# First MLP by Horner's rule with h read from PSUM, GpSimd's arithmetic moved to VectorE

## The chip, the cores and the metric

The kernel runs on one core of one Trainium2 chip. The metric is the device time of one execution in microseconds. All arithmetic is in float32; a product that TensorE forms is made of three matmuls, with each operand split into a rounded high part and a low part (float32r).

## The reference

A linear recurrence over 768 steps in each of 4 x 8 heads gives x, and two MLPs follow, one on the other's result:

```
mag = sqrt(a_re^2 + a_im^2);  a <- a * min(mag, 0.999) / (mag + 1e-6)     # complex
S_re, S_im <- a * S + k v^T  (each step t; kv goes to the real part)
y[t] = q[t] . S_re                                   # [4, 8, 768, 48] -> x [3072, 384]

h = x @ w_in                                         # [3072, 2048]
g = (a0 + a1 h + a2 h^2 + a3 h^3) / (1 + |b0| |h| + |b1| h^2 + 1e-6)
x1 = g @ w_out                                       # [3072, 384]

out = (silu(x1 @ w_gate) * (x1 @ w_val)) @ w_out2    # d_ff = 1536
```

## The kernel before

The 3072 tokens are cut into 12 units of 256 tokens. For each unit an element-wise part works on VectorE, ScalarE and GpSimd: `ew_seed` (the magnitudes' seeds), `ew_scan` (products of the factors), `ew_q` and `ew_k` (the scaled q and k, stored to DRAM by `products`). An attention-like part, `at_units`, then works on chunks of 128 tokens: `at_pre` makes masked products `pm`, `at_post` carries the state `S` and writes x^T into the two parts `xh` and `xl` of a block.

A block is two units, 512 tokens; there are six. For each block `moe` runs the first MLP, 16 steps of 128 columns of d_ff, and the second MLP, 12 steps. One step of the first MLP: `up` makes `ph` = h in PSUM with nine matmuls (L182 to L184); ScalarE and VectorE evaluate numerator `u` and denominator `w`; `r` near 1/w comes from Ln and Exp on ScalarE (L122); `divide` makes `hi` (rounded quotient) and `lo` (its rest); `down` adds nine matmuls to the three accumulators `acc` (L190 with `hi`, L191 with `lo`, L192 with the weights' low part and `hi`). `divide` of a step is called in the step after it (`HALF = 1`), and its `down` one step later again (`pend`, `flush`). A step of the second MLP makes `pg` and `pv` with 18 matmuls, Silu on ScalarE (tile `u`), `z = pv * sg` on VectorE (L270, tile `w`), `hi` on ScalarE (L271) and `lo = z - hi` on GpSimd (L272); its `down` comes after the next step's `up`. The tiles `u`, `w` and `r` have three buffers, `hi` and `lo` two.

After each step `tick` calls the generators of other work, the element-wise part of units two blocks ahead and the attention of the next block, so that it is spread between the steps. Blocks 4 and 5 have no element-wise work left, block 5 no attention. The order on each engine is what the Tile framework's scheduler makes of the order of the calls and the dependencies; each engine then runs its own list in order. SyncE issues all the loads and stores.

In block 0 the weights come as float64 words. `converted` loads them, `to_bits` turns them into float32 with three VectorE instructions (L134 to L136), `narrow` rounds the high part on ScalarE (L143) and takes the low part on GpSimd (L146), and the two parts are stored to DRAM for the later blocks: 40 pieces, 28 of 768 columns and 12 of 384. `TOUCH` makes VectorE write one column of the destination first (L313). Other GpSimd work: `x + z` in `ew_seed` (L458) and `ew_k` (L559) for units 1 to 11, and for units 0 and 1 (`POOL_S`) the mask (L604), the state's sum (L620) and `xl` (L642).

Numerator and denominator of the first MLP are evaluated so:

```
u = a3 h + a2 (ScalarE);  s = h^2 (ScalarE);  w = b0 |h| (ScalarE)
u = u * s (GpSimd, L219);  w = s * b1 + w (VectorE, L220)
u = h * a1 + u (VectorE, L224, reads ph)
divide: hi = (u + a0) r (L232);  w = (w + 1 + eps) hi (L233)
        u = (u + a0) - w (L237);  lo = u r (L238), all VectorE
```

Of the kernel before, what the change touches and what calls it, by code (L numbers as in the profile page):

```python
# [37 lines left out]
POOL_S = range(2)  # L38
# [5 lines left out]
TOUCH = 1  # L44
# [9 lines left out]
LTR = [()] * 6  # L54
# [11 lines left out]
def tile_recurrence_moe(  # L66
# [63 lines left out]
    def to_bits(raw, x):  # L130
        """float64 words in raw to float32's bits in their lower halves; below the normal range these mean nothing."""
        words = raw.bitcast(I32).rearrange("p (n t) -> p t n", t=2)
        low, top = words[:, 0, :], words[:, 1, :]
        v_.tensor_scalar(x, top, 3, 0x3FFFFFFF, ALU.logical_shift_left, ALU.bitwise_and)  # L134
        stt(x, top, -0x40000000, x, ALU.bitwise_and, ALU.bitwise_or)
        stt(low, low, 29, x, ALU.logical_shift_right, ALU.bitwise_or)  # L136
        return top.bitcast(F32), low.bitcast(F32)

    def narrow(raw, x, wt, low_sum):
        """float64 words to float32 in the two parts of wt; low_sum > 0 if one is below the normal range."""  # L140
        t, xf = to_bits(raw, x)
        hi, lo = wt[:, 0, :], wt[:, 1, :]
        act(hi, xf, AF.Copy)  # L143
        act(t, t, AF.Abs)
        act(t, t, AF.Relu, scale=-1.0, bias=cst[:, 4:5], accum_out=low_sum)
        g_.tensor_tensor(lo, xf, hi.bitcast(F32), SUB)  # L146

    def narrow_any(raw, x, wt):
        """As narrow(), with what lies below the normal range taken as zero."""
        t, xf = to_bits(raw, x)  # L150
        act(t, t, AF.Abs)
        v_.tensor_scalar(t, t, WMIN, None, ALU.is_ge)
        tt(xf, xf, t, MUL)
# [19 lines left out]
    def moe(pools, T, x_hi, x_lo, out_ap, tick, middle, take, ltr=()):  # L173
        """x^T [128, KT, T] in two parts to out_ap [128, KT, T] in DRAM."""
# [24 lines left out]
        def flush(n):  # L199
            while len(pend) > n:  # L200
                down(*pend.pop(0))

        acc = [pacc.tile([128, T], F32, tag=f"acc{m}", name="acc") for m in range(KT)]
        for f in range(0, F1, gf):
# [6 lines left out]
            u, s, w, r = (mt(n) for n in ("u", "s", "w", "r"))  # L211
            hi, lo = mt("hi", F32R), mt("lo", F32R)
            L_ = f in ltr
            act(u, ph, AF.Identity, scale=a3, bias=a2)  # L214
            act(s, ph, AF.Square)  # L215
            act(w, ph, AF.Abs, scale=b0)  # L216
            if L_:
                act(r, ph, AF.Identity, scale=a1, bias=a0)
            g_.tensor_tensor(u, u, s, MUL)  # L219
            stt(w, s, b1, w, MUL, ADD)  # L220
            if L_:
                tt(u, u, r, ADD)
            else:
                stt(u, ph, a1, u, MUL, ADD)  # L224
            fact(r, w, AF.Ln, bias=cst[:, 2:3])
            fact(r, r, AF.Exp, scale=-1.0)

            def divide(L_=L_, f=f, wts=wts, u=u, w=w, r=r, hi=hi, lo=lo):
                if L_:
                    tt(hi, u, r, MUL)  # L230
                else:
                    stt(hi, u, a0, r, ADD, MUL)  # L232
                stt(w, w, 1.0 + EPS, hi.bitcast(F32), ADD, MUL)  # L233
                if L_:
                    tt(u, u, w, SUB)
                else:
                    stt(u, u, a0, w, ADD, SUB)  # L237
                tt(lo, u, r, MUL)  # L238
                for j in range(gf):
                    pend.append((acc, wts[j], DM, hi[:, j, :], lo[:, j, :], f + j == 0, f + j == F1 - 1))  # L240
# [17 lines left out]
        for f in range(0, F2, gf):  # L258
# [13 lines left out]
            g_.tensor_tensor(lo, z, hi.bitcast(F32), SUB)  # L272
            for j in range(gf):
                pend.append((acc2, wts[j], 0, hi[:, j, :], lo[:, j, :], f + j == 0, f + j == F2 - 1))
            flush(gf)
            tick(1)
# [26 lines left out]
    def converted(wp, src, scr, f):  # L303
        parts = []
        for c, n in spans(src):
# [6 lines left out]
            if TOUCH:  # L312
                v_.tensor_copy(wt[:, 0, 0:1], cst[:, 0:1])  # L313
# [20 lines left out]
    def general():  # L334
        """The recurrence a step at a time, where a product of its factors leaves float32's range."""
# [89 lines left out]
    with ExitStack() as es:  # L425
# [13 lines left out]
        def cmul(dst, x, y, t):  # L439
            """dst = x * y, all [128, 2, n]; t [128, 2, 2, n]."""  # L440
# [9 lines left out]
        def ew_seed(u):  # L450
# [7 lines left out]
            (g_ if u else v_).tensor_tensor(x, x, z, ADD)  # L458
# [60 lines left out]
        def products(u, i, src):  # L519
            """src * A, or src * A / |A|^2, to DRAM."""  # L520
# [13 lines left out]
        def chunk(u, n):  # L534
            """Q' and K' of a chunk as rows (part, d)."""
# [16 lines left out]
        def ew_k(u):  # L552
# [6 lines left out]
            (g_ if u else v_).tensor_tensor(x, x, z, ADD)  # L559
# [25 lines left out]
        def at_pre(u, n, held):  # L585
            """K'^T and the masked products of K' and Q' of a chunk."""
# [3 lines left out]
            for hh in range(2):  # L590
# [11 lines left out]
                if u in POOL_S:  # L602
                    act(pm, pp, AF.Copy)
                    g_.tensor_tensor(pm, pm, wide, MUL)  # L604
                else:
                    tt(pm, pp, wide, MUL)

        def at_post(u, n, held, xh, xl, col):
            st, vt, S_old = st_of.pop((u, n)), v_of.pop((u, n)), state[0]
            has_s = u % UPB > 0 or n > 0  # L610
            if "kT" in held:
# [5 lines left out]
                if u in POOL_S:  # L617
                    act(S_new, pg, AF.Copy)
                    if has_s:
                        g_.tensor_tensor(S_new, S_new, S_old, ADD)  # L620
                elif has_s:
# [16 lines left out]
            if u in POOL_S:  # L638
                xf = atp.tile([128, KT, 128], F32, tag="ysb", name="xf")
                act(xf, px, AF.Copy)  # L640
                act(xh[:, :, xs], px, AF.Copy)
                g_.tensor_tensor(xl[:, :, xs], xf, xh[:, :, xs].bitcast(F32), SUB)  # L642
            else:
                split(px, xh[:, :, xs], xl[:, :, xs])
# [12 lines left out]
        def at_units(*us):  # L657
            """Chunk by chunk, the first half of one beside the second half of the one before."""
# [45 lines left out]
        def merge(*streams):  # L704
            """(steps, their number) side by side, each spread over the whole."""
# [44 lines left out]
        for i in range(len(BLOCKS)):  # L750
# [43 lines left out]
            moe(pools, T, *xt[i], o, tick, silu, feed(stored, pools[3]) if i else first, LTR[i])  # L794
# [97 lines left out]
```

## Time and profile before

| | |
|---|---|
| three runs | 1402.33, 1409.41, 1424.78 us; median 1409.41 |
| profiled execution: span from first to last instruction | 1421.0 us |
| profiled execution's own time | not listed apart from the three runs; the slowest of them is 3.8 us above the span |
| TensorE matmuls busy | 1142.4 us, 80% |
| VectorE busy | 1142.4 us, 80% |
| ScalarE busy | 676.0 us, 48% |
| GpSimd busy | 408.2 us, 29%, 259 instructions |
| mean granted TensorE clock | 0.938 |

Busy time of an engine includes time in which an instruction has started and stands still. The sixteen DMA engines move 261.55 MB. The stages are told apart by the loads of activation tables: a first MLP needs Ln and Exp, a second one Silu. In order of time they are the start (0 to 170 us), then first and second MLP of blocks 0 to 5: 289.7, 422.1, 569.3, 671.9, 776.2, 870.9, 968.0, 1060.2, 1161.7, 1246.5 and 1333.1 us are the borders.

### The profile page before, as it was taken

Reading aid. Unit: us, or ns where it says so; the run is one execution under the profiler, and the core shown is the slowest. Engines: PE = TensorE matmul, PEld = TensorE weight load, DVE = VectorE, ACT = ScalarE, POOL = GpSimd, SP = SyncE. Lnnn points to the kernel's source line nnn. Section 1 sums busy time; section 2 is a strip of 40 time slices with the busy share of each in tenths; the row PEclk is TensorE's granted clock in tenths of the full one; section 3 lists DMA queues with packets and bytes.
Section 4 is the critical chain, followed back from the end, with each engine's and each line's share of the span. In section 5 each row is a group of like instructions: output and inputs, shape, how many; then the busy total and the mean of one; then the engine's idle time right before and its main releaser. Section 6 shows DMA issues by size and latency. Waiting matters only on the chain. (4 is left out here: it accounts for less than half of the span.)

```text
span 1421.0 us, 15576 instructions
## 1 busy us (share of the span) xinstructions
PE 1142.4 (80%) x5314; PEld 926.9 (65%) x5314; DVE 1142.4 (80%) x1878; ACT 676.0 (48%) x1078; POOL 408.2 (29%) x259
## 2 busy tenths in 40 slices
PE   0041977887679776999899998999989999988897
PEld 0041956675458455887678776788767888866686
DVE  7999689999897999799799896999987871159710
ACT  6454276864453647222865225763226542255421
POOL 2233354334441313022432223221222211123211
PEclk9999979988777997899899999999999999999999
DMA  7666254646565664667754676455756535544551
GB/s 268 231 214 199 94 158 167 212 166 228 199 199 212 170 213 155 195 216 215 242 162 146 206 234 207 156 180 192 226 182 199 163 110 178 170 143 158 181 170 47
DMA packets 129159, 261.55 MB, mean 184 GB/s; under 512 B 8112, under 2 KB 85168, under 8 KB 129072
## 3 DMA queue, kind: packets, MB, share of 16 engines
q1 hardware_dynamic: 129072, 260.47, 56.6%
q8 instruction: 44, 0.72, 0.2%
q14 instruction: 43, 0.35, 0.1%
HBM read 210.11 MB, written 50.33 MB: 183 GB/s over the span
## 5 line engine op out<-in xcount | busy, mean ns | idle before, releaser
L191 PE MATMUL acc<-lo,wt 128*128 128x512 f32 x504 | 220.1, 437 | 78.3 <-DVE lo L238 52.4
L219 POOL TENSOR_TENSOR u<-u,s 128x512 f32<-128x512 f32 x96 | 153.0, 1594 | 364.2 <-ACT s L215 329.4
L272 POOL TENSOR_TENSOR lo<-w,hi 128x512 fp32r<-128x512 f32 x72 | 104.1, 1446 | 387.6 <-ACT hi L271 387.5
L192 PE MATMUL acc<-hi,wt 128*128 128x512 f32 x504 | 211.0, 419 | 0.8 <-POOL wt L146 0.8
L190 PE MATMUL acc<-hi,wt 128*128 128x512 f32 x504 | 181.4, 419 | 32.8 <-DVE hi L232 15.7
L191 PEld LDWEIGHTS acc<-lo,wt 128*128 128x128 f32 x504 | 101.1, 201 | 131.9 <-DVE lo L238 79.7
L270 DVE TENSOR_TENSOR w<-pv,u 128x512 f32<-128x512 f32 x72 | 49.2, 683 | 133.5 <-PE pv L184 133.5
L190 PEld LDWEIGHTS acc<-hi,wt 128*128 128x128 f32 x504 | 99.8, 202 | 63.8 <-DVE hi L232 21.1
L271 ACT ACTIVATE hi<-w 128x512 fp32r<-128x512 f32 x72 | 45.3, 630 | 198.0 <-DVE w L270 197.8
L182 PE MATMUL ph<-xh,wt 128*128 128x512 f32 x288 | 120.9, 422 | 10.4 <-DMA wt<-w1s 6.3
L220 DVE SCALAR_TENSOR_TENSOR w<-s,par,w 128x512 f32<-128x512 f32 x96 | 93.6, 975 | 37.2 <-ACT w L216 36.9
L594 PE MATMUL pk<-ident,st 96*128 96x96 f32 x160 | 23.7, 277 | 119.4 <-DMA st<-qs 119.4
L184 PE MATMUL ph<-xh,wt 128*128 128x512 f32 x288 | 116.8, 406 | 2.5 <-POOL wt L146 2.5
L183 PE MATMUL ph<-xl,wt 128*128 128x512 f32 x288 | 117.1, 407 | 0.0
L146 POOL TENSOR_TENSOR wt<-raw,wt 128x768 fp32r<-128x768 f32 (+1 forms) x40 | 80.2, 2007 | 127.2 <-ACT wt L143 101.8
L192 PEld LDWEIGHTS acc<-hi,wt 128*128 128x128 f32 x504 | 101.9, 202 | 20.1 <-POOL wt L146 1.1
L232 DVE SCALAR_TENSOR_TENSOR hi<-u,par,r 128x512 fp32r<-128x512 f32 x96 | 105.1, 1096 | 11.4 <-PE acc L192 5.6
L214 ACT ACTIVATE u<-ph,par 128x512 f32<-128x512 f32 x96 | 74.5, 776 | 79.0 <-DVE lo L238 53.4
L122 ACT ACTIVATE r<-w,cst 128x512 f32<-128x512 f32 x96 | 69.1, 720 | 80.0 <-DVE w L220 80.0
L182 PE MATMUL pg<-x1h,wt 128*128 128x512 f32 x216 | 91.6, 424 | 12.4 <-ACT wt L143 12.4
L594 PEld LDWEIGHTS pk<-ident,st 96*128 96x128 f32 x160 | 20.9, 167 | 123.1 <-issue 119.8
L184 PE MATMUL pg<-x1h,wt 128*128 128x512 f32 x216 | 90.2, 417 | 6.7 <-POOL wt L146 6.7
(123 smaller groups left out, 2886.4 us busy)
## 6 DMA issues: line engine op xcount, KB each, us to landing
wt<-w1s SPq DMA_DIRECT2D x89, 768.0 KB, 4.3
wt<-w2s SPq DMA_DIRECT2D x60, 768.0 KB, 4.6
wt<-w2s SPq DMA_DIRECT2D x60, 384.0 KB, 4.1
raw<-in_w_p SPq DMA_DIRECT2D x28, 768.0 KB, 5.7
qs<-qp SPq DMA_DIRECT2D x24, 768.0 KB, 4.5
st<-qs SPq DMA_DIRECT2D x96, 192.0 KB, 4.7
w1s<-wt SPq DMA_DIRECT2D x16, 768.0 KB, 4.2
a<-in_a_p SPq DMA_DIRECT2D x12, 768.0 KB, 6.8
```

Of the source, the lines that this page charges most:

```text
L146: g_.tensor_tensor(lo, xf, hi.bitcast(F32), SUB)
L182: t_.matmul(ph, whi, xh[:, k, :], start=(k == 0), stop=False)
L183: t_.matmul(ph, whi, xl[:, k, :], start=False, stop=False)
L184: t_.matmul(ph, wlo, xh[:, k, :], start=False, stop=(k == KT - 1))
L190: t_.matmul(acc[m], whi, hi, start=st, stop=False)
L191: t_.matmul(acc[m], whi, lo, start=False, stop=False)
L192: t_.matmul(acc[m], wlo, hi, start=False, stop=sp)
L214: act(u, ph, AF.Identity, scale=a3, bias=a2)
L219: g_.tensor_tensor(u, u, s, MUL)
L220: stt(w, s, b1, w, MUL, ADD)
L232: stt(hi, u, a0, r, ADD, MUL)
L272: g_.tensor_tensor(lo, z, hi.bitcast(F32), SUB)
```

## The change

The numerator is evaluated by Horner's rule, and both evaluations read h from PSUM: `w = b1 |h|` on ScalarE, `w = (w + b0) h` on VectorE, then Abs on ScalarE, which gives b1 h^2 + b0 |h|; `u = a3 h + a2` on ScalarE, `u = u h` and `u = (u + a1) h` on VectorE. The square `s` is gone. `lo = u r` of the first MLP is GpSimd's, and is all that GpSimd computes apart from constants at the start and end: `narrow`'s low part, `lo` of the second MLP, the sums of `ew_seed` and `ew_k` and all of the `POOL_S` work are VectorE's. In the second MLP the pending `down` and the tick now come before `lo`. `TOUCH`, `POOL_S` and `LTR` (a variant that no block used) are removed.

```
         (narrow)
-        g_.tensor_tensor(lo, xf, hi.bitcast(F32), SUB)
+        tt(lo, xf, hi.bitcast(F32), SUB)
         (moe, first MLP)
-            act(u, ph, AF.Identity, scale=a3, bias=a2)
-            act(s, ph, AF.Square)
-            act(w, ph, AF.Abs, scale=b0)
-            g_.tensor_tensor(u, u, s, MUL)
-            stt(w, s, b1, w, MUL, ADD)
-            stt(u, ph, a1, u, MUL, ADD)
+            act(w, ph, AF.Abs, scale=b1)
+            act(u, ph, AF.Identity, scale=a3, bias=a2)
+            stt(w, w, b0, ph, ADD, MUL)
+            tt(u, u, ph, MUL)
+            act(w, w, AF.Abs)
+            stt(u, u, a1, ph, ADD, MUL)
             (divide)
-                tt(lo, u, r, MUL)
+                g_.tensor_tensor(lo, u, r, MUL)
         (moe, second MLP)
-            g_.tensor_tensor(lo, z, hi.bitcast(F32), SUB)
+            flush(0)
+            tick(1)
+            tt(lo, z, hi.bitcast(F32), SUB)
             for j in range(gf):
                 pend.append(...)
-            flush(gf)
-            tick(1)
         (converted)
-            if TOUCH:
-                v_.tensor_copy(wt[:, 0, 0:1], cst[:, 0:1])
         (ew_seed, ew_k)
-            (g_ if u else v_).tensor_tensor(x, x, z, ADD)
+            tt(x, x, z, ADD)
         (at_pre; at_post likewise for S and xl)
-                if u in POOL_S:
-                    act(pm, pp, AF.Copy)
-                    g_.tensor_tensor(pm, pm, wide, MUL)
-                else:
-                    tt(pm, pp, wide, MUL)
+                tt(pm, pp, wide, MUL)
```

## Rows read from the trace of the kernel before

**Rows 1.** Busy time by stage; stretch, length, engines, then granted clock, DMA share, GB/s.

```profile
0.00:170.00 170.00, 50.58 (x259) 50.24 (x260) 149.41 (x295) 78.53 (x115) 54.48 (x43) 1.00 0.61 207
170.00:289.70 119.70, 90.78 (x365) 69.08 (x365) 104.26 (x126) 84.23 (x136) 50.50 (x28) 0.89 0.55 178
289.70:422.10 132.40, 99.06 (x342) 74.47 (x343) 123.21 (x204) 67.33 (x116) 55.83 (x33) 0.81 0.56 193
422.10:569.30 147.20, 115.59 (x533) 91.00 (x532) 136.63 (x244) 82.23 (x129) 39.60 (x22) 0.85 0.59 189
569.30:671.90 102.60, 101.04 (x526) 86.11 (x526) 90.06 (x191) 26.96 (x42) 19.55 (x12) 0.95 0.66 205
671.90:776.20 104.30, 94.56 (x489) 76.70 (x489) 92.89 (x111) 70.73 (x115) 34.74 (x20) 0.95 0.59 193
776.20:870.90 94.70, 87.31 (x418) 71.06 (x418) 87.01 (x181) 25.68 (x40) 22.05 (x14) 0.98 0.65 204
...
1060.20:1161.70 101.50, 92.26 (x470) 75.07 (x470) 83.19 (x107) 57.45 (x96) 24.57 (x18) 0.97 0.52 161
1161.70:1246.50 84.80, 84.80 (x416) 71.56 (x415) 15.70 (x24) 19.60 (x32) 14.12 (x11) 0.96 0.53 169
1246.50:1333.10 86.60, 71.91 (x295) 54.19 (x294) 75.09 (x92) 51.77 (x86) 27.65 (x17) 0.99 0.44 148
```

**Rows 2.** Timeline of a step, last first MLP: start, duration, engine, line, operation.

```profile
1283.01 1.80 POOL L219 TENSOR_TENSOR u<-u,s 128x512 f32<-128x512 f32 x1 [3.20 <-ACT s L215]
1283.19 0.39 PE L182 MATMUL ph<-xh,wt 128*128 128x512 f32 x1
...
1283.59 1.78 DVE L232 SCALAR_TENSOR_TENSOR hi<-u,par,r 128x512 fp32r<-128x512 f32 x1
...
1285.00 0.39 PE L184 MATMUL ph<-xh,wt 128*128 128x512 f32 x1
1285.29 0.68 DVE L238 TENSOR_TENSOR lo<-u,r 128x512 fp32r<-128x512 f32 x1
1285.89 0.74 DVE L220 SCALAR_TENSOR_TENSOR w<-s,par,w 128x512 f32<-128x512 f32 x1
...
1286.56 0.74 DVE L224 SCALAR_TENSOR_TENSOR u<-ph,par,u 128x512 f32<-128x512 f32 x1
...
1287.22 0.68 DVE L233 SCALAR_TENSOR_TENSOR w<-w,hi 128x512 f32<-128x512 f32 x1
...
1287.93 0.75 DVE L237 SCALAR_TENSOR_TENSOR u<-u,par,w 128x512 f32<-128x512 f32 x1
...
1288.60 1.78 DVE L232 SCALAR_TENSOR_TENSOR hi<-u,par,r 128x512 fp32r<-128x512 f32 x1
```

**Rows 3.** Three VectorE lines: minimum, median, maximum in ns, first and last start.

```profile
L232 DVE SCALAR_TENSOR_TENSOR hi<-u,par,r x96: 735/748/1833, 188.7 to 1333.8; 128x512 fp32r<-128x512 f32 x96
...
L224 DVE SCALAR_TENSOR_TENSOR u<-ph,par,u x96: 735/740/750, 186.8 to 1331.6; 128x512 f32<-128x512 f32 x96
...
L270 DVE TENSOR_TENSOR w<-pv,u x72: 627/685/697, 305.0 to 1408.6; 128x512 f32<-128x512 f32 x72
```

**Rows 4.** Groups by line, 1257 to 1333 us, VectorE's `hi` and GpSimd.

```profile
L232 DVE SCALAR_TENSOR_TENSOR hi<-u,par,r 128x512 fp32r<-128x512 f32 x15 | 25.3, 1687 | 1.1 <-ACT r L122 1.1
...
L219 POOL TENSOR_TENSOR u<-u,s 128x512 f32<-128x512 f32 x16 | 26.4, 1648 | 52.7 <-ACT s L215 52.7
```

**Rows 5.** Groups by line and shape, whole span: busy us, mean ns, idle before.

```profile
L516 DVE TENSOR_TENSOR a<-t,t 128x768 f32<-128x768 f32 x12 | 11.4, 949 | 0.0
L128 DVE TENSOR_TENSOR xl<-px,xh 128x384 fp32r<-128x384 f32 x20 | 11.0, 551 | 5.0 <-ACT xh L127 4.9
...
L313 DVE CAST wt<-cst 128x1 fp32r<-128x1 f32 x40 | 5.4, 144 | 4.2 <-POOL wt L146 4.2
```

**Rows 6.** Timeline of a second MLP step, block 2: TensorE's wait, VectorE's next product.

```profile
805.68 0.50 PE L191 MATMUL acc<-lo,wt 128*128 128x512 f32 x1 [0.62 <-POOL lo L272]
...
809.03 0.69 DVE L270 TENSOR_TENSOR w<-pv,u 128x512 f32<-128x512 f32 x1
```

More of the change, by code (lines that the diff above doesn't have):

```diff
@@ L37 @@
 HP = B * H // 2
-POOL_S = range(2)
 ST_BUFS = 3
@@ L43 @@
 X_BUFS = 1
-TOUCH = 1
 RECIP = range(3, 12)
@@ L53 @@
 M_BUFS = {"hi": 2, "lo": 2}
-LTR = [()] * 6
 HALF = 1
@@ L171, in mag_scale, with moe @@
         stt(m, z, 0.5 * CAP, e, MUL, MIN)
-    def moe(pools, T, x_hi, x_lo, out_ap, tick, middle, take, ltr=()):
+    def moe(pools, T, x_hi, x_lo, out_ap, tick, middle, take):
         ps, pacc, mp, wp, xp = pools
@@ L210, in moe, with divide @@
                 up(ph[:, j, :], wt, 0, x_hi, x_lo)
-            u, s, w, r = (mt(n) for n in ("u", "s", "w", "r"))
+            u, w, r = (mt(n) for n in ("u", "w", "r"))
             hi, lo = mt("hi", F32R), mt("lo", F32R)
-            L_ = f in ltr
+            act(w, ph, AF.Abs, scale=b1)
             act(u, ph, AF.Identity, scale=a3, bias=a2)
-            act(s, ph, AF.Square)
-            act(w, ph, AF.Abs, scale=b0)
-            if L_:
-                act(r, ph, AF.Identity, scale=a1, bias=a0)
-            g_.tensor_tensor(u, u, s, MUL)
-            stt(w, s, b1, w, MUL, ADD)
-            if L_:
-                tt(u, u, r, ADD)
-            else:
-                stt(u, ph, a1, u, MUL, ADD)
+            stt(w, w, b0, ph, ADD, MUL)
+            tt(u, u, ph, MUL)
+            act(w, w, AF.Abs)
+            stt(u, u, a1, ph, ADD, MUL)
             fact(r, w, AF.Ln, bias=cst[:, 2:3])
             fact(r, r, AF.Exp, scale=-1.0)
[L228 to L232, printed above, removed]
-                stt(w, w, 1.0 + EPS, hi.bitcast(F32), ADD, MUL)
[L234 to L237, printed above, removed]
-                tt(lo, u, r, MUL)
+            def divide(f=f, wts=wts, u=u, w=w, r=r, hi=hi, lo=lo):
+                stt(hi, u, a0, r, ADD, MUL)
+                stt(w, w, 1.0 + EPS, hi.bitcast(F32), ADD, MUL)
+                stt(u, u, a0, w, ADD, SUB)
+                g_.tensor_tensor(lo, u, r, MUL)
                 for j in range(gf):
@@ L558, in ew_k @@
             act(t1, a, AF.Square)
-            (g_ if u else v_).tensor_tensor(x, x, z, ADD)
+            tt(x, x, z, ADD)
             if u % UPB == UPB - 1:
@@ L601, in at_pre @@
                 wide = mask[:, None, :].to_broadcast([128, 4, CH])
-                if u in POOL_S:
-                    act(pm, pp, AF.Copy)
-                    g_.tensor_tensor(pm, pm, wide, MUL)
-                else:
-                    tt(pm, pp, wide, MUL)
+                tt(pm, pp, wide, MUL)
         def at_post(u, n, held, xh, xl, col):
@@ L616, in at_post @@
                 S_new = state[0] = atp.tile([R2, DM], F32, tag="S", name="S")
[L617 to L621, printed above, removed]
+                if has_s:
                     tt(S_new, pg, S_old, ADD)
@@ L637, in at_post @@
             xs = slice(col + n * CH, col + (n + 1) * CH)
[L638 to L644, printed above, removed]
+            split(px, xh[:, :, xs], xl[:, :, xs])
             yield
@@ L793, in tile_recurrence_moe @@
             o = out[:, :, starts[i] * U : starts[i] * U + T]
-            moe(pools, T, *xt[i], o, tick, silu, feed(stored, pools[3]) if i else first, LTR[i])
+            moe(pools, T, *xt[i], o, tick, silu, feed(stored, pools[3]) if i else first)
         pgd = ps.tile([128, 2], F32, tag="ps", name="pgd")
```

## Prediction

> **What bounds the kernel now.** I read the stages first: one row of busy times for each stage, cut where the activation tables change [rows 1]. Up to 569.3 us VectorE is busy 149.41 of 170.00, 104.26 of 119.70, 123.21 of 132.40 and 136.63 of 147.20 us, TensorE much less: VectorE sets the pace. In the second MLP of block 1 (569.3 to 671.9) TensorE is busy 101.04 of 102.60 us, in that of block 4 all of 84.80: TensorE is the bound and VectorE's time is cheap. The first MLPs lie between: in block 5's, the last, VectorE has 75.09 of 86.60 us and TensorE 71.91. Block 2's rows stand for block 3's.
>
> Then one step of that last first MLP, where no attention or element-wise work is mixed in [rows 2]. VectorE's starts follow each other without a gap, and the step lasts 5.01 us (`hi` at 1283.59, the next at 1288.60): `hi` 1.70, `lo` 0.60, `w` 0.67, `u` 0.66, `w` 0.71, `u` 0.67. TensorE needs 18 matmuls; the nine from 1283.19 to 1285.00 start 0.226 us apart, so 18 take 4.07 us, and it waits for the rest. The reader should look at `hi`: an instruction of its kind costs 0.67 elsewhere in the step, here 1.70. GpSimd's `u*s` runs from 1283.01 to 1284.81; `hi` ends at 1285.37, 0.56 later, about its own length. VectorE stands still while it counts as busy.
>
> That this is GpSimd's presence and not the instruction is seen in the spread by line [rows 3]: `hi`, both tensors in SBUF, goes from 735 (median 748) to 1833 ns; L224 and L270, which read one tensor from PSUM, stay within 735 to 750 and 627 to 697 ns. In this trace neither of the lines that read PSUM is lengthened. The Trainium skill (SBUF — State Buffer, section "Who interferes with whom") states it as a lock: a VectorE instruction with two SBUF inputs contends with a GpSimd instruction that reads SBUF, and the second to start waits; with one SBUF input it doesn't. The trace agrees (1833 against 750 ns at most).
>
> A price for it: in 1257 to 1333 us GpSimd was busy 26.4 us, with `u*s` alone, and 15 `hi` took 1687 ns instead of 748 [rows 4, 3]: 15 x 0.939 = 14.1 us, so 0.53 us of VectorE for each microsecond of GpSimd, and 0.88 us for each of its 16 products.
>
> **The change part by part.**
> *GpSimd's present work ends.* At 0.53 the lock returns 28.9 + 26.8 + 29.6 + 21.0 = 106 us to VectorE up to 569.3 us (GpSimd's 54.48, 50.50, 55.83, 39.60), 18.4 and 11.7 in block 2's stages, 13.0 in block 4's first MLP [rows 1]. In the second MLPs of blocks 4 and 5 VectorE is idle most of the time, so nothing counts there.
>
> *First MLP.* VectorE's six instructions a step stay six: `u*h` comes, `lo` goes, and `w` and the last `u` of the evaluation read PSUM, at L224's and L270's prices. Without a lock the step is 0.67 + 0.60 + 0.66 + 0.67 + 0.71 + 0.67 = 3.98 us. On ScalarE an Abs replaces the Square, one for one; it waits for VectorE's `w`, and behind it are this step's Ln and Exp, which waited for the same `w` before: nothing new waits. Two inputs more from PSUM: `pv*sg` takes 685 ns (median), `u*r` from SBUF 0.68 us [rows 3, 2], so I cost that at nothing. The Trainium skill (VectorE: DVE Perf Modes, section "The TRN2 errata — SBUF-src ops pay a fixed extra latency per instruction") speaks against it: 120 fixed cycles from PSUM against 58 from SBUF. An estimate from that page is 65 ns for each of 192 instructions, 12 us less gain; the trace shows about 5 ns.
>
> *The product that GpSimd keeps,* `lo = u*r`, 96 times. It starts when VectorE's last `u` ends. If VectorE's next instructions read PSUM, it costs nothing; if they are element-wise work of the recurrence, it costs as `u*s` does, 0.88 us, and I take no more. Blocks 0 to 3 have such work behind each step: 0.88. Blocks 4 and 5 have none, and the three that read PSUM take some 1.9 us together, longer than the 1.65 us mean of `u*s` [rows 4]: I take a quarter, 0.22 us, for orders where `hi` or `w` falls on it. Bounds for all: 0 and 0.88. Its latency is some 1.0 us longer than VectorE's (1.65 against 0.68), and three buffers of `u` and `r` wait for it before ScalarE refills them; while VectorE or TensorE sets the step, this is hidden; if not, it is 1.0 us a step, 16 us in each first MLP.
>
> *Work that comes to VectorE.* The weights' low parts: 28 of 768 columns and 12 of half, at 0.949 and 0.551 (L516 and L128, [rows 5]): 33.2 us, all before 422 us. 22 sums in the seeds and keys at 0.949, half of them before 569 us: 10.4. Eight masked products at 0.68 and seven small ones at 0.55: 9.3. `lo` of the second MLP, 12 x 0.68 = 8.2 a block. The 40 one-column copies go, 0.144 each: -5.8. Before 569.3 us this is 33.2 + 10.4 + 9.3 + 8.2 - 5.8 = 55 us. The stores of converted weights, issued by SyncE, now wait for VectorE instead of GpSimd; behind them are only loads that run ahead, cost nothing.
>
> *New waits.* Where VectorE subtracts what ScalarE has just rounded, it waits today 0.25 us (4.9 over 20, [rows 5]): 40 narrowings, 10 us; above, a rounding pass each as long as VectorE's own at this width, 0.949, 38 us (an estimate); below, as much as 10 us gained, because waits for GpSimd's weights and sums end too. I take nothing: the 10 us lost are the nearest row, and the 10 us that may be gained balance them.
>
> *Sum, on the profiled span of 1421.0 us.* Up to 569.3 us: -106 + 55 + 32 x 0.88 = -23 us of VectorE, which is 90% of the time there: -21. First MLPs of blocks 2 and 3: -18.4 + 14.1 + 1.9 = -2.4 each, -5. Second MLPs of both: -11.7 + 10.1 = -1.6 each, -3. Block 1's second MLP: TensorE, nothing. Block 4's first MLP: -13.0 + 3.5 = -9.5, but TensorE is idle for only 9.2 us of it; half, -5. Block 5's: 3.98 + 0.22 = 4.20 instead of 5.01 a step, 15 steps, -12; TensorE's 4.07 is next. In all -46 us: 1375. The span lies 11.6 us above the median of the three runs, so I carry the share over: 1409.41 x 1375/1421 = 1364 us. The granted clock, 0.81 to 0.89 between 170 and 569 us [rows 1], may rise if TensorE waits less; I don't count it.
>
> **The rivals.**
> *The lock moves with the product* (B). All 96 cost 0.88 and the narrowings wait half of the upper bound (19 us). Blocks 4 and 5 then gain 0 and 2 instead of 17, so 31 - 19 = 12 us: 1397, no change that can be measured (2% is about what can be told). For it: the product has the same width and engine as `u*s`. Against: half of the step's instructions now read PSUM, one of six before.
>
> *No lock at all* (C). All products fall beside PSUM reads: the first stages gain 25 more, blocks 2 and 3 five to ten each until TensorE binds, blocks 4 and 5 seven: -88 us, 1322. Against: the element-wise work behind the steps reads SBUF.
>
> *`lo` of the second MLP comes too late* (D), the slower case. It now stands behind a tick's work in VectorE's queue. In one step of block 2 TensorE waited 0.62 us for GpSimd's `lo` and went on at 805.68; VectorE finished the work before its next `pv*sg` at 809.03 [rows 6], so a `lo` behind that work is ready at 809.7, 4 us later. TensorE's next accumulations and, behind them in its queue, the matmuls of the next step but one wait. Blocks 0 to 3 have 48 such steps; the gain is gone at 0.96 us a step, and at 2 us a step the time is 1421 - 46 + 96, 1459 for the median. Against: where VectorE is the bound, TensorE's wait is slack already, and in block 2 VectorE has 87.01 of 94.70 us. It decides only in stages where TensorE has no slack left, as in block 1.
>
> **How the numbers follow.** Forecast 0.50 (1335 to 1385 by itself), B 0.22, C 0.15, D 0.13. The range runs from below C to the upper part of B, 1310 to 1425, leaving out D and a few per cent of tails. Faster by over 2% (under 1381): most of the forecast and C, 0.59; within 2%: B and the forecast's upper end, 0.27; slower: D, 0.14.
>
> **What would show it.** GpSimd's busy time falls to some 150 us in 96 products. L232's and L237's successors have medians near 0.75 us and few long ones; if the long ones are as many as now, B holds. The last first MLP's step is 4.1 to 4.3 us and TensorE no longer waits there for `lo`. In the second MLPs of blocks 1 to 3 the wait of the accumulation for `lo` stays under 10 us a block; much more is D. Stages up to 569.3 us together shorten by some 20 us. The prediction is wrong if the scheduled order puts SBUF work behind every product, or if VectorE, waiting for ScalarE, loses what the lock returns.

## The result, and the profile after

The changed kernel takes 1339.67 us (median of four executions, 1336.88 to 1346.15), the kernel before, run beside it, 1405.87 us (1401.09 to 1424.78). The ratio is 0.953, with a 95% interval of 0.946 to 0.960: faster, inside the range, 24 us below the forecast.

The first two parts of the page of the kernel after, busy time by engine and the granted clock:

```profile
span 1335.0 us, 15523 instructions
PE 1105.1 (83%) x5314; PEld 902.9 (68%) x5314; DVE 1074.8 (81%) x1987; ACT 679.5 (51%) x1063; POOL 144.9 (11%) x110
PEclk9999779999797898999998999999999999999899
```

The profiled execution took 1336.88 us, 1.9 us more than its span. Executions of one kernel differ by more than some of the effects below: the profile of [rows 1] is of the slowest of before's four (1424.78 us, span 1421.0), and those of h_copy and lo2_gpsimd are of executions at a lower clock that their ratios leave out. The stages are therefore compared with a second profile of the kernel before (1403.64 us, span 1401.4; experiment before_again). The same view as [rows 1] for it, cut where the activation tables change: stretch, length, busy time of TensorE, weight loads, VectorE, ScalarE and GpSimd with counts, granted clock, DMA share, GB/s.

```profile
0.00:280.90 280.90, 132.21 (x623) 110.47 (x623) 256.77 (x421) 162.44 (x251) 104.26 (x71) 0.94 0.60 201
280.90:410.50 129.60, 98.09 (x342) 73.61 (x343) 123.11 (x205) 67.41 (x115) 55.69 (x33) 0.80 0.57 197
410.50:551.20 140.70, 109.74 (x533) 85.86 (x532) 135.40 (x244) 82.25 (x129) 39.23 (x22) 0.89 0.62 196
...
649.70:757.00 107.30, 97.69 (x489) 79.86 (x489) 92.14 (x111) 70.75 (x116) 33.47 (x20) 0.92 0.57 187
757.00:854.30 97.30, 91.23 (x418) 74.87 (x418) 87.06 (x181) 25.63 (x39) 21.74 (x14) 0.93 0.64 199
...
1226.70:1313.30 86.60, 73.22 (x294) 55.48 (x293) 75.12 (x92) 51.75 (x86) 27.68 (x17) 0.97 0.45 148
```

The same stages of the kernel after (start with block 0's first MLP, block 0's second, block 1's first, block 2's two, block 5's first):

```profile
0.00:260.90 260.90, 127.72 (x596) 104.22 (x596) 222.41 (x431) 152.29 (x228) 27.31 (x28) 0.93 0.63 208
260.90:377.00 116.10, 91.77 (x369) 70.98 (x370) 109.52 (x205) 69.18 (x117) 5.05 (x3) 0.88 0.70 236
377.00:528.00 151.00, 113.99 (x544) 90.41 (x543) 141.24 (x279) 86.61 (x134) 21.36 (x15) 0.85 0.59 187
...
621.80:717.90 96.10, 88.94 (x476) 73.45 (x474) 84.90 (x117) 70.95 (x113) 21.39 (x15) 1.00 0.61 195
717.90:806.70 88.80, 88.22 (x424) 74.11 (x423) 76.32 (x188) 25.46 (x40) 2.75 (x2) 0.94 0.69 212
...
1164.10:1242.00 77.90, 70.50 (x289) 52.91 (x287) 69.33 (x92) 53.76 (x85) 17.99 (x14) 0.98 0.48 157
```

Read down the lengths and then VectorE's busy time, the third with a count behind it: where a stage is shorter, VectorE is busy for less. Some element-wise work has moved from second to first MLPs (block 1's first VectorE instructions: 244 before, 279 after), so sums over blocks say more than single stages:

| stages | before, us | after, us | difference | forecast |
|---|---|---|---|---|
| start, block 0, block 1's first MLP | 551.2 | 528.0 | -23.2 | -21 |
| block 1's second MLP | 98.5 | 93.8 | -4.7 | 0 |
| blocks 2 and 3, first MLPs | 204.5 | 192.4 | -12.1 | -5 |
| blocks 2 and 3, second MLPs | 189.5 | 171.2 | -18.3 | -3 |
| block 4, both MLPs | 183.0 | 178.7 | -4.3 | -5 |
| block 5, both MLPs | 174.7 | 170.9 | -3.8 | -12 |
| sum | 1401.4 | 1335.0 | -66.4 | -46 |

To see the lock itself I use one number throughout, the *lengthening*: for each VectorE instruction that overlaps an arithmetic instruction of GpSimd, its duration less the median of those of its line and shape that overlap none, summed over the trace. It is 204.8 us before and 40.3 us after.

A step of the last first MLP after the change, which answers to [rows 2] (VectorE, GpSimd and TensorE's first accumulation; columns as there):

```profile
1197.88 0.73 DVE L212 SCALAR_TENSOR_TENSOR w<-w,par,ph 128x512 f32<-128x512 f32 x1
...
1198.54 0.74 DVE L222 SCALAR_TENSOR_TENSOR u<-u,par,w 128x512 f32<-128x512 f32 x1
...
1199.20 0.67 DVE L213 TENSOR_TENSOR u<-u,ph 128x512 f32<-128x512 f32 x1
...
1199.44 1.29 POOL L223 TENSOR_TENSOR lo<-u,r 128x512 fp32r<-128x512 f32 x1 [3.30 <-ACT w L214]
...
1199.80 1.48 DVE L220 SCALAR_TENSOR_TENSOR hi<-u,par,r 128x512 fp32r<-128x512 f32 x1
...
1200.79 0.50 PE L188 MATMUL acc<-lo,wt 128*128 128x512 f32 x1 [0.43 <-POOL lo L223]
...
1201.20 0.73 DVE L215 SCALAR_TENSOR_TENSOR u<-u,par,ph 128x512 f32<-128x512 f32 x1
...
1204.38 1.49 DVE L220 SCALAR_TENSOR_TENSOR hi<-u,par,r 128x512 fp32r<-128x512 f32 x1
```

`hi` at 1199.80, the next at 1204.38: the step is 4.58 us, 5.01 before. GpSimd's `lo` starts behind VectorE's `u` of L222 and runs to 1200.73. One instruction that reads PSUM, `u*ph`, lies beside it and keeps its 0.67 us; the next in the queue is `hi`, with two tensors in SBUF, and it stands still until `lo` ends: 1.48 instead of 0.75.

Minimum, median and maximum by line after the change, which answer to [rows 3]:

```profile
L220 DVE SCALAR_TENSOR_TENSOR hi<-u,par,r x96: 648/752/1762, 163.8 to 1245.1; 128x512 fp32r<-128x512 f32 x96
L212 DVE SCALAR_TENSOR_TENSOR w<-w,par,ph x96: 731/737/748, 157.5 to 1239.2; 128x512 f32<-128x512 f32 x96
L213 DVE TENSOR_TENSOR u<-u,ph x96: 624/676/683, 159.1 to 1240.5; 128x512 f32<-128x512 f32 x96
L215 DVE SCALAR_TENSOR_TENSOR u<-u,par,ph x96: 732/735/749, 160.5 to 1242.5; 128x512 f32<-128x512 f32 x96
```

None of the three lines that read `ph` from PSUM has a long instance in 96; `hi` has, 34 of its 96 by over 0.2 us, and `hi` holds 26.3 us of the 40.3.

### The profile page after: what moved, and what is told of

Same layout as the page of the kernel before. It is cut to its first block, busy times and chain, and to the rows that moved or that the text cites. A ratio compares the mean times of both kernels' runs of the same rounds, so it can differ in the third digit from the quotient of the medians.

```text
span 1335.0 us, 15523 instructions
## 1 busy us (share of the span) xinstructions
PE 1105.1 (83%) x5314; PEld 902.9 (68%) x5314; DVE 1074.8 (81%) x1987; ACT 679.5 (51%) x1063; POOL 144.9 (11%) x110
## 5 line engine op out<-in xcount | busy, mean ns | idle before, releaser
L188 PE MATMUL acc<-lo,wt 128*128 128x512 f32 x504 | 216.2, 429 | 58.8 <-POOL lo L223 50.0
L223 POOL TENSOR_TENSOR lo<-u,r 128x512 fp32r<-128x512 f32 x96 | 144.2, 1502 | 1104.8 <-DVE u L222 790.2
L189 PE MATMUL acc<-hi,wt 128*128 128x512 f32 x504 | 207.1, 411 | 0.0
L187 PE MATMUL acc<-hi,wt 128*128 128x512 f32 x504 | 176.8, 411 | 13.8 <-DVE hi L220 12.6
L188 PEld LDWEIGHTS acc<-lo,wt 128*128 128x128 f32 x504 | 100.5, 199 | 106.6 <-POOL lo L223 75.1
L255 DVE TENSOR_TENSOR w<-pv,u 128x512 f32<-128x512 f32 x72 | 49.3, 685 | 104.9 <-PE pv L181 104.9
L119 ACT ACTIVATE u<-pg 128x512 f32<-128x512 f32 x72 | 43.0, 598 | 129.2 <-PE pg L181 128.9
L220 DVE SCALAR_TENSOR_TENSOR hi<-u,par,r 128x512 fp32r<-128x512 f32 x96 | 97.6, 1017 | 13.9 <-ACT r L119 8.7
L210 ACT ACTIVATE w<-ph,par 128x512 f32<-128x512 f32 x96 | 65.7, 684 | 78.0 <-PE ph L181 58.0
L179 PE MATMUL pg<-x1h,wt 128*128 128x512 f32 x216 | 89.3, 413 | 7.8 <-ACT wt L140 7.8
L212 DVE SCALAR_TENSOR_TENSOR w<-w,par,ph 128x512 f32<-128x512 f32 x96 | 70.9, 739 | 30.4 <-ACT u L211 30.3
L181 PE MATMUL pg<-x1h,wt 128*128 128x512 f32 x216 | 87.2, 404 | 3.4 <-DVE wt L143 3.4
L180 PE MATMUL pg<-x1l,wt 128*128 128x512 f32 x216 | 87.5, 405 | 0.7 <-DVE x1l L125 0.7
L179 PEld LDWEIGHTS ph<-xh,wt 128*128 128x128 f32 x288 | 57.6, 200 | 44.7 <-ACT wt L140 16.3
```

Of the source, the lines that this page charges most:

```text
L179: t_.matmul(ph, whi, xh[:, k, :], start=(k == 0), stop=False)
L180: t_.matmul(ph, whi, xl[:, k, :], start=False, stop=False)
L181: t_.matmul(ph, wlo, xh[:, k, :], start=False, stop=(k == KT - 1))
L187: t_.matmul(acc[m], whi, hi, start=st, stop=False)
L188: t_.matmul(acc[m], whi, lo, start=False, stop=False)
L189: t_.matmul(acc[m], wlo, hi, start=False, stop=sp)
```

## The experiments

Ratios are to the kernel before, run on the same chip beside each kernel; a time "by ratio" is the ratio times 1405.87 us. The kernel after, at 0.953, is 1340 us by its ratio.

**before_again.** The kernel before, unchanged, for a second profile.

> The kernel before, unchanged, for a second profile: the span of the profile shown (1421.0 us) is that of the slowest of its executions, and that of the changed kernel (1335.0) of the fastest. If stages differ from the first profile by the 15 to 20 us that the execution times differ by, the borders of the stages say where that lies: spread over all stages (the TensorE clock, about 1% each) or in the start and block 0 alone, where transfers and conversions run.

Measured: 1403.64 us. Its stages are the table's. Of the 19.6 us between the two spans 18.1 lie before the end of block 1's first MLP, spread over its stages. The lengthening is 204.8 us, in the first profile 202.9: what the lock takes hardly differs between the two.

**moves_only and poly_only.** The change in its two halves. moves_only leaves the polynomial as it was (GpSimd keeps `u*s`) and moves the rest:

```diff
-POOL_S = range(2)
+POOL_S = ()
-TOUCH = 1
+TOUCH = 0
-        g_.tensor_tensor(lo, xf, hi.bitcast(F32), SUB)
+        tt(lo, xf, hi.bitcast(F32), SUB)
...
-            g_.tensor_tensor(lo, z, hi.bitcast(F32), SUB)
+            flush(0)
+            tick(1)
+            tt(lo, z, hi.bitcast(F32), SUB)
...
-            flush(gf)
-            tick(1)
...
-            (g_ if u else v_).tensor_tensor(x, x, z, ADD)
+            tt(x, x, z, ADD)
```

poly_only is the kernel before with the diff's first MLP alone (Horner from `ph`, `g_.tensor_tensor(lo, u, r, MUL)`).

> All moves from GpSimd to VectorE, and the second MLP's new order, but the first MLP's polynomial left as before (u*s on GpSimd, lo on VectorE). Theory, the lock: the lengthening of VectorE's lines outside the first MLP's own six goes (about 118 of 203 us), 90 us of work comes in loaded stages, so some 28 us less, 1375 to 1390. Rival, the chain: the gain is the path through GpSimd's u*s in the first MLP; it is still there, so nothing is gained, 1400 to 1410. Rival, the waits: the gain is TensorE's waits for low parts that GpSimd made in the conversions and the second MLP; all of the gain is here, 1340 to 1350.

> The polynomial's part alone: Horner from PSUM, lo of the first MLP on GpSimd, GpSimd keeping all its other work. Theory, the lock: 0.9 us for each u*s becomes 0.4 for each lo, 45 us of VectorE in first MLPs, some 35 to 40 us less, 1365 to 1375. Rival, the chain: the whole gain, 1340 to 1350. Rival, the waits: nothing, 1400 to 1410.

Measured: moves_only 1372.65 us, ratio 0.972 (0.965 to 0.978), lengthening 84.0 us; poly_only 1392.2 us, ratio 0.987 (0.982 to 0.992), lengthening 160.4 us. By ratio -40 and -18 us, -58 in sum, against -66 for both. So the gain is not the polynomial's alone and not the moves' alone. The moves take 121 us out of the lengthening, the polynomial 44 (204.8 to 160.4), whether the moves are made or not (84.0 to 40.3). What it is worth differs: 18 us by itself, 27 on top of the moves (0.972 to 0.953). moves_only took a little less than was expected of it (1375 to 1390), poly_only more (1365 to 1375). In poly_only the lengthening went as expected, 44 us for 45, and the time didn't follow: up to the end of block 1 it is 5.7 us behind the kernel before (655.4 against 649.7), and only blocks 2 to 5 are shorter, by 20.3; VectorE, busy for 44 us less, stands idle 29 us more. Which wait that is isn't located. What stayed with GpSimd goes on lengthening VectorE there, 31.3 us in block 0's second MLP and 11.5 to 12.2 in those of blocks 1 to 3. In moves_only GpSimd has `u*s` alone, and `hi` shows the lock undiminished (spread by line of moves_only):

```profile
L232 DVE SCALAR_TENSOR_TENSOR hi<-u,par,r x96: 732/742/1833, 172.7 to 1288.2; 128x512 fp32r<-128x512 f32 x96
```

84.0 us over 96 products is 0.88 us each, the price that the prediction read from [rows 4]. Its last first MLP is 86.0 us long, like before's 86.6; poly_only's is 78.7, like after's 77.9.

**all_vector.** The last product on VectorE as well, so that GpSimd has no arithmetic at all.

```diff
-                g_.tensor_tensor(lo, u, r, MUL)
+                tt(lo, u, r, MUL)
```

> The changed kernel with its last GpSimd product, lo of the first MLP, on VectorE as well: GpSimd computes nothing. Theory, the lock: no VectorE line is lengthened (39 us back) and 96 instructions of 0.6 us come, 58 us: 10 to 20 us slower than the changed kernel, 1345 to 1360, and the last first MLP's step equals the 4.58 us that it has now. Rival, offloading: what counts is work taken from VectorE, GpSimd's time is free: 58 us slower, 1385 to 1400.

Measured: 1347.53 us, ratio 0.956 (0.950 to 0.961). By ratio 4 us above the kernel after, by the medians 8; the intervals overlap. GpSimd's product saves VectorE 96 x 0.683 = 66 us of work (the median of `lo` there is 683 ns) and costs it 40 us of standing still, and what is left is hardly to be measured. Its last first MLP is as long as the kernel after's, 77.6 us against 77.9, as expected. The spread of `hi` by line, all_vector: with GpSimd silent there is no long one.

```profile
L220 DVE SCALAR_TENSOR_TENSOR hi<-u,par,r x96: 651/745/753, 165.4 to 1259.3; 128x512 fp32r<-128x512 f32 x96
```

**extra_read and extra_write.** More work for GpSimd that nobody waits for, once reading SBUF and once only writing to it.

```diff
+    junk = cpool.tile([128, 4, 128], F32, name="junk")
...
                 g_.tensor_tensor(lo, u, r, MUL)
+                wide = mask[:, None, :].to_broadcast([128, 4, 128])
+                g_.tensor_tensor(junk, wide, wide, MUL)
```

```diff
+    junk = cpool.tile([128, 4, 128], F32, name="junk")
...
                 g_.tensor_tensor(lo, u, r, MUL)
+                g_.memset(junk, 1.0)
+                g_.memset(junk, 1.0)
```

> The changed kernel with one more GpSimd product behind each lo of the first MLP (96 of them, 128x512, both inputs the mask in SBUF, its output used by nothing), so GpSimd computes twice as long, but on no path. Theory, the lock: each costs VectorE 0.3 to 0.7 us as lo does (40 us for 96 in the changed kernel), so VectorE's lengthening rises from 40 to 70 to 110 us and the time by 20 to 50 us, to 1360 to 1390. Rival, paths: GpSimd only matters through what waits for its results; nothing waits for this one, so 1337 to 1345.

> As the run with the extra product, but GpSimd only writes: two memsets of 128x512 behind each lo, about as long. Theory, the lock on the read side (the Trainium skill, SBUF — State Buffer, section Who interferes with whom, says that a GpSimd instruction that only writes does not contend with an instruction of two SBUF inputs): VectorE is not lengthened beyond the changed kernel's 40 us, 1337 to 1350. Rival, any GpSimd activity holds VectorE up: as the extra product, 1360 to 1390.

Measured: extra_read 1414.16 us, ratio 1.007 (1.004 to 1.010), some 77 us above the kernel after; extra_write 1342.62 us, ratio 0.955 (0.951 to 0.959), the same as after. Spread by line of extra_read:

```profile
L226 POOL TENSOR_TENSOR junk<-mask x96: 1038/1233/2434, 5.5 to 144.8; 128x512 f32<-128x512 f32 x96
```

Its first stage, columns as in the stages above:

```profile
0.00:331.50 331.50, 132.35 (x596) 106.78 (x596) 297.04 (x431) 152.95 (x228) 158.67 (x124) 0.93 0.50 164
```

and the spread of one of the two memsets of extra_write:

```profile
L225 POOL MEMSET junk<- x96: 524/524/892, 1.0 to 114.1; 128x512 f32 x96
```

The extra instructions wait for nothing, and all of them ran at the start, beside element-wise work that reads SBUF only. So extra_read is slower than was expected (1360 to 1390), and what it tells of is the start. There the 96 reads are 133.1 us of GpSimd; VectorE's lengthening in the stage goes from 6.5 to 81.6 us, the stage from 260.9 to 331.5, and the later stages keep their lengths within 2 us, but for block 1's second MLP (93.8 to 101.9). That is 75.1/133.1 = 0.56 us of VectorE for each microsecond of GpSimd, beside the 0.53 from [rows 4]. The 192 memsets put some 102 us on GpSimd in the same place (246.6 us busy against 144.9) and leave the lengthening at 41.8 us; with VectorE's instructions beside the memsets counted too, it is 2.6 us more. For instructions with two SBUF inputs it is GpSimd's reads that VectorE waits for, not its being busy, as the Trainium skill (SBUF — State Buffer, section "Who interferes with whom") has it.

Two SBUF inputs are not the only case, though. The first instruction of `to_bits` reads one SBUF tensor, `raw`, and does not go beyond 560 ns where GpSimd has no arithmetic (all_vector). Beside GpSimd's reads it reaches 1391 ns, and beside the memsets 971 (extra_read, then extra_write):

```profile
L132 DVE TENSOR_SCALAR x<-raw x40: 347/550/1391, 13.5 to 443.2; 128x768 int32<-128x768 int32 x28, 128x384 int32<-128x384 int32 x12
L132 DVE TENSOR_SCALAR x<-raw x40: 346/549/971, 12.5 to 375.5; 128x768 int32<-128x768 int32 x28, 128x384 int32<-128x384 int32 x12
```

A copy of one SBUF tensor of 128x6 (L478) takes up to 1001 and 597 ns in the same two traces. Most of the 2.6 us is of these one-input kinds. So the prediction's words "with one SBUF input it doesn't" hold for the two lines that it shows, whose other input is in PSUM, and not for every instruction with one SBUF input.

**h_copy and h_sbuf.** ScalarE copies `ph` to SBUF; h_copy leaves the copy unused, h_sbuf reads it in the three VectorE instructions in the place of `ph`.

```diff
+            hs = mt("hs")
+            act(hs, ph, AF.Copy)
-            stt(w, w, b0, ph, ADD, MUL)
-            tt(u, u, ph, MUL)
+            stt(w, w, b0, hs, ADD, MUL)
+            tt(u, u, hs, MUL)
             act(w, w, AF.Abs)
-            stt(u, u, a1, ph, ADD, MUL)
+            stt(u, u, a1, hs, ADD, MUL)
```

(h_copy: the first two lines alone.)

> Control for the next run: the changed kernel with a ScalarE copy of h from PSUM to an SBUF tile in each step of the first MLP that nothing reads (96 of about 0.6 us, on an engine that is busy half of the time). Either theory: 1340 to 1360.

> The same copy, and VectorE's three instructions of the evaluation read h from it instead of from PSUM, so all six of a step have two SBUF inputs. Theory, the lock: the three lines, which now never exceed 750 ns, get maxima of 1.5 us and more, the lengthening rises from 40 to some 80 us, and the time is 20 to 40 us above the control's. Rival, the price of PSUM (a fixed extra cost of a PSUM source, about 65 ns by the Trainium skill, VectorE: DVE Perf Modes, section on the TRN2 errata): the three lines are 65 ns shorter each, 288 of them, up to 19 us below the control.

Measured: h_copy 0.957 (0.951 to 0.963), 1345 us by its ratio; h_sbuf 1382.06 us, 0.980 (0.977 to 0.984). The spread of the first of the three lines, h_copy:

```profile
L214 DVE SCALAR_TENSOR_TENSOR w<-w,par,ph x96: 728/742/750, 166.0 to 1270.4; 128x512 f32<-128x512 f32 x96
```

and the first two of h_sbuf:

```profile
L214 DVE SCALAR_TENSOR_TENSOR w<-w,par,hs x96: 651/745/1850, 167.6 to 1289.3; 128x512 f32<-128x512 f32 x96
L215 DVE TENSOR_TENSOR u<-u,hs x96: 622/681/1785, 169.2 to 1290.0; 128x512 f32<-128x512 f32 x96
```

Two things follow. A PSUM input costs these instructions nothing that shows: 742 ns against 745, and 676 in the kernel after against 681. The Trainium skill (VectorE: DVE Perf Modes, section "The TRN2 errata — SBUF-src ops pay a fixed extra latency per instruction") gives 120 fixed cycles for a PSUM source against 58 from SBUF; no row here shows a difference, and the prediction was right to go by its rows. And with SBUF in PSUM's place the same instructions reach 1785 and 1850 ns, the lengthening is 77.8 us, and the kernel takes 33 us more than its control by the ratios. Waiting for the copy is no rival for this: before the first of the three lines VectorE waits 15.8 us for ScalarE in h_sbuf, 30.3 in the kernel after. So 33 us is what Horner's reading `h` from PSUM is worth in this order of work.

**grouped.** Ties `hi` behind the next step's last instruction that reads PSUM, so that all three lie beside GpSimd's product.

```diff
-            stt(u, u, a1, ph, ADD, MUL)
+            third = stt(u, u, a1, ph, ADD, MUL)
...
-                stt(hi, u, a0, r, ADD, MUL)
+                order(stt(hi, u, a0, r, ADD, MUL), last[0])
...
+            last[0] = third
```

> The changed kernel with one ordering edge for VectorE: hi of a step behind the last PSUM-reading instruction of the next step, so two instructions that read PSUM (1.3 us) follow the u that releases GpSimd's lo, where now one (0.6 us) and then hi follow. Theory, the lock: in the last first MLP hi's 1.48 us falls to some 1.0 and the step from 4.58 to about 4.1, the lengthening from 40 to 15 to 25 us, the time by 5 to 15 us to 1325 to 1335. Rival, order: VectorE then waits for TensorE and ScalarE where the scheduler had filled the time, 1340 to 1360.

Measured: 1337.69 us, ratio 0.953 (0.948 to 0.958), no change against the kernel after. Its step (timeline of the last first MLP, grouped):

```profile
1194.74 0.74 DVE L222 SCALAR_TENSOR_TENSOR u<-u,par,w 128x512 f32<-128x512 f32 x1
...
1195.41 0.68 DVE L213 TENSOR_TENSOR u<-u,ph 128x512 f32<-128x512 f32 x1
1195.66 1.30 POOL L223 TENSOR_TENSOR lo<-u,r 128x512 fp32r<-128x512 f32 x1 [2.79 <-ACT w L214]
1196.12 0.75 DVE L215 SCALAR_TENSOR_TENSOR u<-u,par,ph 128x512 f32<-128x512 f32 x1
1196.79 0.75 DVE L220 SCALAR_TENSOR_TENSOR hi<-u,par,r 128x512 fp32r<-128x512 f32 x1
```

Two PSUM reads now cover `lo`, `hi` has its 0.75, and the step is 4.09 us (1196.79 to 1200.88), TensorE's 4.07 but for 0.02. The stage shrinks from 77.9 to 73.3 us, its lengthening from 10.3 to 0.8. The step was right, the whole not (1325 to 1335 was expected, 1340 to 1360 by the rival; 1340 by the ratio): over the whole trace the lengthening is some 30 us, not 15 to 25. And what the later stages gain the first ones lose: up to the end of block 1's first MLP grouped takes 534.4 us, the kernel after 528.0, and from there on 798.7 against 807.0, in the profiled executions. In the first part VectorE is busy 4.3 us more (477.5 against 473.2); the start alone has 25 of its instructions more, block 1's first MLP 24 fewer. Why the first part is longer isn't located.

**divide_first.** The recurrence's part ahead of the evaluation's VectorE part, in the program's order.

```diff
             act(u, ph, AF.Identity, scale=a3, bias=a2)
+            if len(half) >= HALF:
+                flush(0)
+                half.pop(0)()
             stt(w, w, b0, ph, ADD, MUL)
...
             half.append(divide)
-            if len(half) > HALF:
-                flush(0)
-                half.pop(0)()
```

> The changed kernel with divide of the step before called ahead of the evaluation of a step instead of behind it. The scheduler then puts two PSUM reads or hi behind u by turns. Theory, the lock: lengthening 25 to 35 us instead of 40, 1330 to 1342. Rival, order: what counts is that hi and lo come earlier for TensorE; its wait for lo (50 us) falls by half and the time by 20 us or more.

Measured: 1322.24 us, ratio 0.941 (0.937 to 0.946), the fastest of all, some 16 us below the kernel after. Its interval lies just below the kernel after's (0.946 to 0.960). Its lengthening is 26.6 us (`hi` 11.5 us with 16 long ones, in place of 26.3 with 34). TensorE's wait for `lo` is no shorter (waits by waiter and releaser: us in total, times, longest; divide_first):

```profile
PE acc L188 <- POOL lo L226: 53.3, 41, 4.8
```

and the kernel after:

```profile
PE acc L188 <- POOL lo L223: 50.0, 61, 4.2
```

The time is nearer to the rival's (20 us or more) than to the theory's (1330 to 1342), but an earlier `lo` is not what it gains by. VectorE's standing still is 14 us less, close to the gain; but the profiled execution of divide_first took 1329.78 us, and the stages don't match one by one (block 0 is 14 us longer, block 1 5.5 shorter, the rest 15 shorter), so how much of the gain is the lock's stays open.

**lo_before_tick and lo2_gpsimd.** The second MLP's `lo` ahead of the tick in VectorE's queue, and on GpSimd.

```diff
             act(hi, z, AF.Copy)
+            tt(lo, z, hi.bitcast(F32), SUB)
             flush(0)
             tick(1)
-            tt(lo, z, hi.bitcast(F32), SUB)
```

```diff
-            tt(lo, z, hi.bitcast(F32), SUB)
+            g_.tensor_tensor(lo, z, hi.bitcast(F32), SUB)
```

> The changed kernel with lo of the second MLP called before the pending accumulation and the tick's work instead of after. Theory (VectorE is the bound there, so TensorE's wait is slack): TensorE's wait for this lo (8.5 us) falls, VectorE's wait for ScalarE's hi (16.2 us) rises, the time is within 10 us, 1335 to 1350. Rival D of the prediction (lo late behind the tick's work costs time): 15 us or more faster, under 1325.

> The changed kernel with lo of the second MLP back on GpSimd (72 products), all else as changed. Theory, the lock: 48 of them, in blocks 0 to 3, meet element-wise work and cost VectorE 0.5 to 0.9 us each, 24 to 43 us, while 33 us of VectorE's own work go: within 15 us, 1335 to 1355. Rival, offloading: 33 us of VectorE less in stages that it bounds, 1310 to 1325.

Measured: lo_before_tick 1342.89 us, ratio 0.956 (0.951 to 0.961), the same as after. The wait that it was to remove, TensorE's for this `lo`, is short in the kernel after:

```profile
PE acc L188 <- DVE lo L259: 8.5, 4, 6.2
```

8.5 us in four waits, 6.2 in one of them; in lo_before_tick that line is gone, and nothing is gained. lo2_gpsimd: 1380.15 us, ratio 0.980 (0.974 to 0.986), 39 us above after. That is above both expectations (1335 to 1355, and 1310 to 1325). Its lengthening is 82.2 us, 42 more, while 49.3 us of VectorE's work left, so VectorE is busy as in the kernel after, 1074.8 us (lo2_gpsimd):

```profile
PE 1142.8 (82%) x5314; PEld 931.3 (67%) x5314; DVE 1076.7 (77%) x1915; ACT 680.7 (49%) x1063; POOL 253.8 (18%) x182
```

Handing 72 subtractions to GpSimd frees VectorE of nothing. It doesn't explain 39 us of time either; TensorE's waits for this `lo`, 8.5 us in the kernel after, may be a part of that (lo2_gpsimd):

```profile
PE acc L188 <- POOL lo L259: 22.4, 16, 3.8
```

The remainder isn't located.

## Why the prediction was right, and where its sizes were off

The forecast of 1364 us was 24 too high. The range, 1310 to 1425, would have held B's 1397 and C's 1322 as well, so that the time fell into it says little; what follows goes by the mechanism.

*The bound, and the lock as cause.* Right. VectorE's busy time falls by 69.2 us, the span by 66.4. all_vector (no long `hi` without GpSimd), extra_read (GpSimd's reads put back, 0.56 us each, time lost) and extra_write (GpSimd busy but not reading, 2.6 us of lengthening and no time lost) show the mechanism from three sides.

*What the lock returns.* The prediction's price, 0.53 us for each microsecond of GpSimd, times GpSimd's work gives 106 + 60 + 13 + 15 us; the lengthening in the same stages of the second profile is 112.6 + 52.7 + 13.1 + 15.3. Right.

*What the product that stays costs: the term that was mis-sized.* It was put at 64 x 0.88 + 32 x 0.22 = 63 us; measured are 40.3. In blocks 0 to 3 it is 25.0 us over 64, 0.39 each, not 0.88: also where element-wise work is queued, the product often falls beside instructions that read PSUM (53 of the 64 have one beside them), and 28 of the 64 cost less than 0.2 us. In block 4 it is 4.1 us, 0.26 each. In block 5 it is 11.2 us, 0.70 each instead of 0.22: the prediction let all three PSUM reads lie beside `lo`, and the scheduled order puts one there and then `hi`. So the step is 4.58 us, not 4.1 to 4.3; grouped shows the 4.09 that the assumed order gives. The error of 23 us in the term is about the 24 us by which the forecast was too high; the other errors, below, go both ways and nearly cancel, which is luck.

*Work that comes to VectorE.* 55 us before the end of block 1's first MLP; measured as VectorE's busy time less the lengthening, 515.3 - 112.6 = 402.7 us before and 473.2 - 15.0 = 458.2 after, +55.5. Right. Blocks 2 and 3: 24 us expected, 15 measured, 9 too many; some work has moved between stages, so neither figure is that of the moved instructions alone.

*The new waits.* Taken as nothing, between 10 us gained and 38 lost. In the first three stages of the table above VectorE is idle 35.9 us before (length less busy time) and 54.8 after (VectorE busy 515.3 and 473.2): 19 us lost, inside the bounds but not for the reason named. The narrowing, L143, waits 3.4 us for ScalarE in all; the largest new wait up to 528 us is attention's, for TensorE (waits of the kernel after up to 528 us, us, times, longest):

```profile
DVE pm L585 <- PE pp L581: 14.0, 5, 5.5
DVE t L441 <- ACT t L440: 9.1, 2, 5.6
...
DVE wt L143 <- ACT wt L140: 3.4, 5, 2.2
```

The first of these was 0.4 us before. So the first row of the stage table, -21 forecast and -23.2 measured, is right by errors that cancel: 13 us less for the product (28.2 expected, 15.0 measured) and 7 more from the lock, against 19 of new waits.

*Blocks 2 and 3.* Here the forecast failed by most: -8 against -30.4. VectorE's account is -52.7 (lock gone) + 10.0 (the product's) + 15 (work) = -28, where the prediction had -60 + 28 + 24 = -8. The product's price is 18 of the difference.

*Block 5.* -12 against -3.8. 15 steps save 0.43 us each, 6.5, not 12, and the first MLP is 8.7 us shorter in all (86.6 to 77.9). Of that 5.5 are lost between the load of Silu's table and the second MLP's first matmul (1242.0 to 1253.4 us after, 1313.3 to 1319.2 before), as the last section shows.

*The signs it named.* GpSimd's 144.9 us in 96 products, the first row of the table and TensorE's 8.5 us for the second MLP's `lo` came as said. The step of 4.58 us did not, and TensorE still waits for `lo` in the last first MLP: 6.0 us in 13 waits, 11.7 in 12 before. The sign for B, as many long ones as now, misleads: `hi` is long by over 0.2 us 34 times after and 35 before, and yet B's time did not come. What went is the lengthening of the other instructions of the step, 48.0 us in L220, L237 and L233 before and 4.5 in L221 and L222 after; and most of that outside the first MLPs, which moves_only shows by itself.

*Rival B* (the lock moves along with the product) holds in block 5 almost, and nowhere else. *Rival C* (no lock at all) would have been 1322; the kernel after is between it and the forecast. divide_first's 1322.24 is C's time without C's mechanism, for 26.6 us of lengthening are left in it. *Rival D* (`lo` of the second MLP too late) falls: 8.5 us of TensorE's waits in the whole trace, the second MLPs of blocks 1 to 3 shorter by 23 us together, and lo_before_tick gains nothing. Of the long wait that D feared there is no trace.

## What to carry to other kernels

Element-wise work that GpSimd takes over isn't free for VectorE: where VectorE runs instructions with two SBUF inputs, a GpSimd instruction that reads SBUF cost it 0.53 to 0.56 us for each of its own microseconds here, and some VectorE instructions with one SBUF input were held up as well. Before handing work over, compare that with what VectorE would need itself (0.68 us against 0.88 lost, for one 128x512 product). What GpSimd did beside VectorE's PSUM reads, and what only wrote, cost VectorE next to nothing here; so give it that, and check in the timeline which instruction is next in VectorE's queue when GpSimd's begins. The order of issue alone was worth 16 us more (divide_first), for a reason that isn't shown in full.

## What the runs showed of the hardware that was not expected

One small instruction can be held up for many times its length. `gd` of 128x3, one SBUF tensor read, takes 155 to 169 ns in the kernel after; in the second profile of the kernel before each of its four instances begins while a GpSimd product runs, takes 1.21 to 1.81 us and ends 22 to 27 ns behind that product. GpSimd is held up as well: the same extra product of extra_read takes from 1038 to 2434 ns.

The place of an instruction in the program does not say when it runs. The 96 extra products of extra_read, which wait for nothing, have all begun by 144.8 us, in the stretch where VectorE is the bound, and gave back all that the change had gained. The order is the scheduler's, not the chip's.

TensorE's granted clock fell to about the lower of its two levels, 1.2 GHz, at the end of the last first MLP: 0.55 and 0.51 in two stretches. Windows of the kernel after there, columns as above:

```profile
1242.00:1246.00 4.00, 3.91 (x9) 2.81 (x9) 2.73 (x5) 1.29 (x2) 0.03 (x1) 0.55 0.34 134
1246.00:1249.00 3.00, 0.75 (x4) 0.62 (x4) 2.75 (x3) 0.00 (x0) 1.59 (x2) 1.00 0.81 255
1249.00:1252.20 3.20, 3.20 (x10) 2.48 (x9) 0.00 (x0) 0.28 (x1) 1.23 (x1) 0.51 0.10 19
1252.20:1262.00 9.80, 9.80 (x44) 7.85 (x43) 3.48 (x6) 3.35 (x6) 0.00 (x0) 0.99 0.73 237
```

TensorE had waited 1.78, 1.44 and 2.25 us for GpSimd's last `lo`s (at 1237.51, 1242.09 and 1248.30); in two stretches its matmuls then start 0.43 us apart, 0.23 before and after. The second profile of the kernel before has one such stretch, 1311.2 to 1315.2 us, granted 0.57, after a wait of 2.62 us. Some 8 more matmuls at 0.2 us extra each are some 1.6 us of the 5.5 that block 5 gave back. Beside these the trace shows a chain: VectorE's last `hi` waits 1.27 us for the accumulations before it (0.31 before), the last `u` is held up by GpSimd's `lo` (1.63 us instead of 0.74), and the last `lo` takes GpSimd 1.27 us, VectorE 0.69.
